# Five down products of block one in full float32, with their weights split a block later

## The chip, the core and the metric

The kernel runs on one core of a Trainium2 chip. The core has TensorE (PE, with its weight loads as PEld), VectorE (DVE), ScalarE (ACT), GpSimd (POOL) and SyncE (SP, whose queue issues most transfers). The metric is the device time of one execution in microseconds, and the median over several runs is compared.

## The reference

2048 tokens of 448 channels go through a conditioned state-space layer and a gated feed-forward layer, each with a residual:

```python
mod = (_silu(c) @ w_mod).reshape(c.shape[0], 6, 1, -1)
sa, ca, ga, sb, cb, gb = (mod[:, 0], mod[:, 1], mod[:, 2], mod[:, 3], mod[:, 4], mod[:, 5])
h = _layernorm(x, axis=-1) * (1 + ca) + sa
x = x + ga * _A_ref(h, ...)          # long convolution over the tokens, as a state-space kernel
h = _layernorm(x, axis=-1) * (1 + cb) + sb
x = x + gb * _B_ref(h, B_w_gate, B_w_up, B_w_down)
...
def _B_ref(x, w_gate, w_up, w_down):  # 448 -> 1792 -> 448
    g = _silu(x @ w_gate)
    u = x @ w_up
    return (g * u) @ w_down
```

Nearly all arithmetic is in `_B_ref`.

## The kernel before

**Products in parts.** The matmuls take operands in a reduced float32 format (F32R, "fp32r" in the profile). To keep float32 accuracy, a value a is split into a high part (a cast by ACT) and a low part (a minus the high part, a subtraction on DVE), and a product is the sum of three matmuls: high by high, high by low, low by high.

**Blocks and pieces.** After a first stage of about 34 us, which computes the modulation and the first tiles of the state-space layer, the 16 tiles of 128 tokens are worked off in eight blocks of two tiles (`run_blocks`, `ffn`). A block runs over 14 pieces f of the 1792 hidden channels, 128 each. Piece f consists of
- the gate and up products (`gate_up`): 42 matmuls with 256 columns, 64 rows each; gate runs on the upper half of the array's rows and up on the lower half, in pairs. The weights of a piece stand as a tile `gu` with a high and a low half; the activations as `hhi` and `hlo`. In block one the order is high by high, high weights by low activations, and the low weights last;
- the gating: ACT's Silu writes `p`, DVE multiplies it by the up product (into the PSUM bank), ACT casts the result to `phi`, DVE subtracts for `plo`;
- the down product (`down`): six slots, three for each of the two tiles, of 64 rows by 448 columns on each half of the array. It is asked for one half in the following piece and the other half in the piece after that (`begin`, `half`, `rest`); `point(f)` puts both between the gate and up matmuls of piece f, before the last two of them (in pieces 1 to 12 of block one).

**Weights in block one.** Gate and up weights of piece j (448 KB) are loaded into one of three staging tiles `raw`, j modulo 3 (`load_w`). `split_w(j, 0)` is ACT's cast into the high half, issued in the gating of piece j-2; the low half follows by `split_w(j, 1)`, a subtraction on DVE at the end of piece j-2. For the pieces in `ADDED` (5, 7, 9, 11, 13) the low half is made another way, `split_w(j, 2)` in the gating of piece j-3: ACT writes the negated weights' copy, and then POOL issues a transfer that adds the staging tile to it and rounds on the way. Hence the low half costs DVE nothing there. Note that the high half must be cast as well:

```python
if fresh and f + 3 in ADDED:
    split_w(f + 3, 2)
if nw is not None:
    split_w(nw, 0)
```

with `nw` = f + 2 in block one, which `fresh` marks. Down weights (224 KB a piece) go through three tiles `rawd` into `wdh` (ACT's cast) and `wdl` (DVE's subtraction, in the gating of their own piece). All split weights stay in SBUF for blocks two to eight, which load no weights.

**Order around it.** Each engine works off its instructions in the order in which they are issued. `PLANS` sets, for each block, after which piece the steps of the next block's tiles are issued: letters are steps (a, b, r, h, v: the convolution's operands; c, p: POOL's skip product and skip addition, at L1005 and L1008; u, w, m, M: statistics of the second norm; X, Y: normalising; T: transposition and stores to DRAM; U: loads of the turned rows into staging tiles), and digits the tile in the block. A plus puts steps inside the gating. In block one tile 0's `c0` stands after piece 4, `c1` and `p0` after piece 5, `p1` after piece 7, T1 after piece 10 and U1 after piece 12. The turned rows become the next block's `hhi` and `hlo` (`split_turned`).

Of the kernel before, what the change touches and what calls it, by code (L numbers as in the profile page):

```python
# [18 lines left out]
L, D, N, F = 2048, 448, 256, 1792  # L19
# [4 lines left out]
NF = F // 128  # L24
# [3 lines left out]
NS = 3  # L28
# [3 lines left out]

ADDED = (5, 7, 9, 11, 13)
PLANS = (
    """pre: s0 ; mid: t0 R0 f s1 ; a0 +g G ; b0 t1 ; r0 h0 R1 ; v0 a1 ; A0 b1 c0 ; B0 c1 e0 p0 ; r1 h1 v1 u0 w0 +E0 M0 ; X0 Y0 p1 ; A1 T0 ;
    B1 E1 m1 ; +M1 X1 Y1 T1 ; +U0 ; U1 e1 L0 ; L1""",
# [17 lines left out]
def f32(ap):  # L56
    return ap.bitcast(F32)
# [3 lines left out]
def tile_kernel(ctx, tc, x, a_re, a_im, b_re, b_im, c_re, c_im, log_dt,  # L61
                wd, wgate_up, states, groups, vecs, dft, idft, out):
    nc = tc.nc
    sy, ve, sc, po, pe = nc.sync, nc.vector, nc.scalar, nc.gpsimd, nc.tensor
# [50 lines left out]
    def split_d(j, part=None):  # L115
        hi, lo = wp[j]
        if not part:
            sc.copy(hi, wdn[j])
        if part != 0:
            ve.tensor_tensor(lo, wdn[j], f32(hi), op=OP.subtract)  # L120

    def split_w(j, part):
        w = raw[j]
# [13 lines left out]
    end = slice(96, 128)  # L137
# [62 lines left out]
    n1, n2 = Norm("a"), Norm("b")  # L200
# [60 lines left out]
    wp0 = ctx.enter_context(tc.tile_pool(name="wp0", bufs=1))  # L261
# [38 lines left out]
    with tc.tile_pool(name="pre", bufs=1) as pre:  # L300
# [4 lines left out]
        for kind, q in ((n[0], n[1:]) for n in ORDER.split()):  # L305
            if kind == "s":
                S[q] = pre.tile([128, NS_], F32, name="s" + q)
                sy.dma_start(S[q], states["abcdef".index(q)])
            elif kind == "m":
                g, b = int(q[0]), (slice(0, 2 * D), slice(2 * D, NM))[int(q[1])]  # L310
                if g not in wms:
                    wms[g] = pre.tile([128, NM], F32, name=f"wm{g}")
                sy.dma_start(wms[g][:, b], groups[g][:, b])
            else:
                {"x": load_x, "w": lambda j: load_w(wp0, j), "d": lambda j: load_d(wp0, j)}[kind](int(q))
        ar, ai, br, bi, cr, ci = (S[q] for q in "abcdef")


# [44 lines left out]
        t1, t2, t3, t4 = (pre.tile([128, NS_], F32, name=q) for q in ("t1", "t2", "t3", "t4"))  # L363
# [117 lines left out]
        def flag_of():  # L481
# [4 lines left out]
        k0, k1 = CV[:, 0:D], DN[2][:, 0:D]  # L486
# [45 lines left out]
            "d00": do(split_d, 0, 0),  # L532
# [212 lines left out]

    def run_blocks(pools, stages, first=None):
        work, hid = pools.work, pools.hid
        rest, ahead, leaving, gate_ready = [], [], [], []

        def both(top, low):  # L750

# [8 lines left out]
        def ffn(b, ts, fresh, last, todo):  # L760
            n, sums = 256, SUMS[b % 2]
            pp = {}
# [9 lines left out]
                return ps, [[(t[:, 0:n], *o) for t in ps] for o in ops]  # L772

            def gating(f, ps, nw):
                p = hid.tile([128, 256], F32, name="p") if fresh else p_of[f % 2]
                hi = hid.tile([128, 256], F32R, name="phi")
                lo = hid.tile([128, 256], F32R, name="plo")
                for g, a in todo.get(-2, []) if f == 0 else []:
                    g(*a)
                gate_ready[:] = [sc.activation(p, ps[0][:, 0:n], AF.Silu).ins.name]  # L780
# [17 lines left out]
                ve.tensor_tensor(lo, ps[1][:, 0:n], f32(hi), op=OP.subtract)  # L798
# [4 lines left out]
                if fresh:  # L803
                    sc.copy(wp[f + 1][0], wdn[f + 1])

            def down(f, q, z):

                hi, lo = pp[f]
                wh, wl = wp[f]
                u, v = ((hi, wh), (hi, wl), (lo, wh))[z]  # L810
                return sums[q][:, 0:D], u[:, cols(q)], v

            def begin(f):

                def half(c, fresh_, end):
                    return [[(*down(f, q, z), fresh_ and z == 0, end and z == 2) for z in range(3)] for q in (c, 1 - c)]

                rest.append((half(1 - f % 2, False, f == (NF - 3 if last else NF - 1)), [leave] if f == NF - 1 else None))
                return half(f % 2, f == 0, False)
# [92 lines left out]
                    pools.load(f + 2 + NS, f + NS)  # L912
            ahead[:] = [begin]

        for j in range(NP0, NP0 + NS - 1):
            pools.load(j)
        if first is not None:
# [18 lines left out]
        def steps(b, nx):  # L936
# [9 lines left out]
                  "o": lambda q: n1.stat(later[q], later), "O": lambda: n1.root(later), "G": gate_row, "g": gate_0, "f": first_rows,  # L946
# [203 lines left out]
```

## Time and profile before

| | us |
|---|---|
| median of 3 runs | 471.24 (471.05 to 471.61) |
| profiled execution, its own time | 471.01 |
| its span, first to last instruction | 469.0 |
| block one, first matmul to block two's first | 33.99 to 97.89 |
| PE busy over the span | 450.2 |
| DVE, ACT, POOL busy | 293.2, 163.6, 105.8 |
| mean granted clock of TensorE | 0.991 |

Busy time is what the instructions of an engine covered; matmuls overlap, so a busy PE is not necessarily at its peak. In rows of the timeline the first number is the start, the second the length, both in us; in square brackets stand the idle time of the engine just before and the engine that ended it. "x2" means that two neighbouring instructions are one row.

### The profile page before, as it was taken

The numbers are of one execution on the slowest core, as the hardware profiler recorded it, in microseconds if no ns is written. First come the engines' busy times: TensorE is split into PE (matmuls) and PEld (weight loads), VectorE is DVE, ScalarE is ACT, GpSimd is POOL, SyncE is SP. The second block draws the span as 40 slices with busy tenths as digits, with TensorE's granted clock in tenths as the row PEclk, the third lists the DMA queues.
The fourth block names the chain that finished last, engine by engine and source line by source line (L and its number), as shares of the span: only waits on it lengthen the run. The fifth ranks groups of instructions, "written<-read, shape, count | busy, mean of one in ns | idle before, by whom it ended". The sixth has DMA issues, their size and how long they took to land.

```text
span 469.0 us, 14543 instructions
## 1 busy us (share of the span) xinstructions
PE 450.2 (96%) x6355; PEld 430.5 (92%) x6355; DVE 293.2 (63%) x600; ACT 163.6 (35%) x395; POOL 105.8 (23%) x132
## 2 busy tenths in 40 slices
PE   6889979889999999999999999999999999999995
PEld 4548978889999999999999999999999999999995
DVE  4889878567664756656755657566755666443324
ACT  5876656442223322232223222232223222222211
POOL 1232423103600242022501142032401152000000
PEclk9999989899999999999999999999999999999999
DMA  8963857732022010302021011202021101202001
GB/s 305 407 231 100 246 160 193 197 77 79 3 61 60 22 61 21 101 1 81 2 74 48 28 55 40 82 3 81 2 81 41 41 4 47 74 3 77 9 1 45
DMA packets 19769, 38.01 MB, mean 81 GB/s; under 512 B 3313, under 2 KB 13169, under 8 KB 19697
## 3 DMA queue, kind: packets, MB, share of 16 engines
q1 hardware_dynamic: 18336, 34.53, 22.9%
q0 software_dynamic: 720, 2.29, 2.9%
q8 instruction: 51, 0.84, 0.7%
q10 hardware_dynamic: 640, 0.18, 0.2%
q14 instruction: 22, 0.17, 0.1%
HBM read 27.76 MB, written 6.88 MB: 74 GB/s over the span
## 4 chain that ended last, share of the span: by engine, by line
PE 81%; DVE 6%; DMA 4%; ACT 3%; issue 3%; POOL 1%; SPq 1%; DVEq 0%; POOLq 0%; ACTq 0%
PE bank L757 50%; PE dn L757 28%; DMA raw<-in_B_w_gate_up_dram 2%; DVE gu L127 1%; DMA raw<-xd 1%; DMA vec<-in_c_log_dt_dram 1%; DVE bank L792 1%; PE dn L489 1%; SPq L252 1%; ACT gu L125 1%; ACT gu L129 1%; DVE sta L161 0%; PE dn L856 0%; PE dn L389 0%; POOL rsa L190 0%
## 5 line engine op out<-in xcount | busy, mean ns | idle before, releaser
L757 PE MATMUL bank<-hhi,gu 64*128 64x256 f32 x3136 | 230.6, 276 | 7.4 <-DVE gu L127 3.7
L757 PEld LDWEIGHTS bank<-hhi,gu 64*128 64x128 f32 x3136 | 210.6, 185 | 9.7 <-DVE gu L127 4.3
L757 PE MATMUL bank<-hlo,gu 64*128 64x256 f32 x1568 | 137.3, 276 | 0.0
L757 PEld LDWEIGHTS bank<-hlo,gu 64*128 64x128 f32 x1568 | 123.0, 186 | 0.3
L780 ACT ACTIVATE raw<-bank 128x256 f32<-128x256 f32 x98 | 37.7, 385 | 190.1 <-PE bank L757 190.1
L792 DVE TENSOR_TENSOR bank<-raw,bank 128x256 f32<-128x256 f32 x91 | 38.9, 427 | 99.9 <-ACT raw L780 99.9
L757 PE MATMUL dn<-wdh,phi 64*128 64x448 f32 x440 | 93.1, 365 | 0.2 <-ACT p L780 0.2
L757 PE MATMUL dn<-wdh,plo 64*128 64x448 f32 x440 | 92.8, 363 | 0.0
L757 PE MATMUL dn<-wdl,phi 64*128 64x448 f32 x440 | 92.6, 362 | 0.0
L798 DVE TENSOR_TENSOR plo<-bank,phi 128x256 fp32r<-128x256 f32 x104 | 44.0, 423 | 29.5 <-ACT phi L797 29.5
L797 ACT CAST phi<-bank 128x256 fp32r<-128x256 f32 x104 | 38.8, 373 | 66.1 <-DVE bank L792 66.1
L757 PEld LDWEIGHTS dn<-wdh,plo 64*128 64x128 f32 x440 | 53.7, 186 | 2.4 <-DVE plo L798 1.4
L757 PEld LDWEIGHTS dn<-wdh,phi 64*128 64x128 f32 x440 | 53.5, 186 | 2.4 <-ACT phi L797 0.7
L757 PEld LDWEIGHTS dn<-wdl,phi 64*128 64x128 f32 x440 | 53.7, 186 | 0.4
L983 POOL TENSOR_TENSOR m<-m,gm 128x448 f32<-128x448 f32 x12 | 13.9, 1156 | 78.2 <-issue 44.2
L190 POOL TENSOR_SCALAR rsa<-mva 128x2 f32<-128x2 f32 (+1 forms) x10 | 6.1, 609 | 89.9 <-DVE mva L162 89.2
L190 POOL TENSOR_SCALAR rsb<-mvb 128x1 f32<-128x1 f32 x16 | 3.5, 219 | 75.4 <-DVE mvb L162 74.8
L259 DVE TENSOR_TENSOR hlo<-raw,hhi 128x512 fp32r<-128x512 f32 (+1 forms) x28 | 16.3, 622 | 2.3 <-ACT hhi L258 1.4
L1005 POOL TENSOR_TENSOR m<-m,gd 128x448 f32<-128x448 f32 x14 | 16.5, 1204 | 0.0
L127 DVE TENSOR_TENSOR gu<-raw,gu 128x896 fp32r<-128x896 f32 x9 | 13.4, 1489 | 3.0 <-ACT gu L125 3.0
L258 ACT CAST hhi<-raw 128x512 fp32r<-128x512 f32 (+1 forms) x28 | 14.6, 565 | 1.5 <-DMA raw<-xd 1.5
L216 DVE SCALAR_TENSOR_TENSOR m<-m,rsb,sb 128x448 f32<-128x448 f32 x14 | 13.8, 983 | 0.8
(214 smaller groups left out, 446.2 us busy)
## 6 DMA issues: line engine op xcount, KB each, us to landing
raw<-in_B_w_gate_up_dram SPq DMA_DIRECT2D x14, 448.0 KB, 3.6
raw<-xd SPq DMA_DIRECT2D x28, 224.0 KB, 3.6
rawd<-in_B_w_down_dram SPq DMA_DIRECT2D x16, 224.0 KB, 3.9
xd<-m SPq DMA_DIRECT2D x56, 56.0 KB, 1.7
x<-in_A_u_dram SPq DMA_DIRECT2D x12, 224.0 KB, 2.7
out_dram<-x SPq DMA_DIRECT2D x11, 224.0 KB, 2.0
wm<-in_w_mod_groups_dram SPq DMA_DIRECT2D x5, 448.0 KB, 8.2
gu<-raw POOLq DMA_DIRECT2D x5, 448.0 KB, 5.8
```

Source lines behind the costliest of these rows:

```text
L127: ve.tensor_tensor(wgu[j][:, 1], w, f32(wgu[j][:, 0]), op=OP.subtract)
L190: po.tensor_scalar(rs[:, 0:n], self.mv[:, 0:n, 1], EPS, None, op0=OP.add)
L216: ve.scalar_tensor_tensor(to, to, rs, sb, op0=OP.mult, op1=OP.add)
L258: sc.copy(hi, src)
L259: ve.tensor_tensor(lo, src, f32(hi), op=OP.subtract)
L757: done.append(pe.matmul(o, w[e], r[e], start=start, stop=stop).ins)
L780: gate_ready[:] = [sc.activation(p, ps[0][:, 0:n], AF.Silu).ins.name]
L792: ve.tensor_tensor(ps[1][:, 0:n], p, ps[1][:, 0:n], op=OP.mult)
L797: sc.copy(hi, ps[1][:, 0:n])
L798: ve.tensor_tensor(lo, ps[1][:, 0:n], f32(hi), op=OP.subtract)
L983: en.tensor_tensor(v, h, g, op=OP.mult)
L1005: po.tensor_tensor(h, h, gd, op=OP.mult)
```

## The change

Pieces 4, 6, 8, 10 and 12 (`WHOLE`) are computed in block one without splitting their down operands. DVE writes their gated product back into `p`, in float32, and the down product is one float32 matmul for each tile and array half, with the weights as they were loaded. Their weights have a tile of their own each, so that they stay until block two. There the new step `W` (`split_whole`) splits them, ACT's cast and DVE's subtraction, after pieces 2, 3, 5, 7 and 9, before the first use in pieces 5, 7, 9, 11 and 13. `ADDED` is empty: the low halves of pieces 5, 7, 9, 11 and 13 are made by DVE like the others, at the end of piece j-2. `p` of block one stands in one tile of its own with two places. The other staging tiles of down weights are counted over the nine remaining pieces.

```diff
-ADDED = (5, 7, 9, 11, 13)
+ADDED = ()
+WHOLE = (4, 6, 8, 10, 12)
...
-    """d0 R0 a0 b0 d1 R1 ; +l0 r0 h0 k0 ; +l1 v0 k1 ; A0 a1 b1 c0 ; B0 p0 e0 E0 c1 ; r1 h1 m0 M0 p1 ; +v1 X0 Y0 L0 L1 ; A1 T0 U0 ; B1 E1 m1 M1 ; +X1 Y1 T1 U1 ; e1 ; ; o0 ; o1 O""",
+    """d0 R0 a0 b0 d1 R1 ; +l0 r0 h0 k0 ; +l1 v0 k1 W4 ; W6 A0 a1 b1 c0 ; B0 p0 e0 E0 c1 ; W8 r1 h1 m0 M0 p1 ; +v1 X0 Y0 L0 L1 ; W10 A1 T0 U0 ; B1 E1 m1 M1 ; W12 +X1 Y1 T1 U1 ; e1 ; ; o0 ; o1 O""",
...
     def load_d(pool, j):
-        wdn[j] = stage_d[j % NS]
-        wp[j] = [pool.tile([128, D], F32R, name=f"wd{q}{j}") for q in "hl"]
+        if j in WHOLE:
+            wp[j] = [pool.tile([128, D], F32R, name=f"wdh{j}")]
+            wdn[j] = pool.tile([128, D], F32, name=f"wd{j}", tag="whole", bufs=len(WHOLE))
+        else:
+            wp[j] = [pool.tile([128, D], F32R, name=f"wd{q}{j}") for q in "hl"]
+            wdn[j] = stage_d[[k for k in range(NF) if k not in WHOLE].index(j) % NS]
...
+    def split_whole(pool, j):
+        a = dict(tag="spare") if j == WHOLE[0] else dict(tag="whole", bufs=len(WHOLE))
+        wp[j].append(pool.tile([128, D], F32R, name=f"wdl{j}", **a))
+        split_d(j)
...
-                p = hid.tile([128, 256], F32, name="p") if fresh else p_of[f % 2]
+                whole = fresh and f in WHOLE
+                if fresh and f == 0:
+                    first_p.append(pools.w.tile([128, 2, 256], F32, name="p", tag="spare"))
+                p = first_p[0][:, f % 2] if fresh else p_of[f % 2]
...
-                ve.tensor_tensor(ps[1][:, 0:n], p, ps[1][:, 0:n], op=OP.mult)
-                if fresh:
+                ve.tensor_tensor(p if whole else ps[1][:, 0:n], p, ps[1][:, 0:n], op=OP.mult)
+                if fresh and not whole:
                     split_d(f, 1)
...
-                sc.copy(hi, ps[1][:, 0:n])
-                ve.tensor_tensor(lo, ps[1][:, 0:n], f32(hi), op=OP.subtract)
+                if whole:
+                    pp[f] = p,
+                else:
+                    sc.copy(hi, ps[1][:, 0:n])
+                    ve.tensor_tensor(lo, ps[1][:, 0:n], f32(hi), op=OP.subtract)
...
-                if fresh:
+                if fresh and f + 1 not in WHOLE:
                     sc.copy(wp[f + 1][0], wdn[f + 1])
...
-                hi, lo = pp[f]
-                wh, wl = wp[f]
-                u, v = ((hi, wh), (hi, wl), (lo, wh))[z]
+                hi, lo = pp[f][0], pp[f][-1]
+                wh, wl = wp[f][0], wp[f][-1]
+                u, v = ((hi, wh), (hi, wl), (lo, wh))[z] if len(pp[f]) > 1 else (hi, wdn[f])
```

In the new order line numbers are 9 to 19 higher. First, DVE in block one from the end of piece 3 to piece 5 (`gu_609` before and `gu_608` after are piece 6's weights; `gu_539` piece 5's; L983 or L1002 is step b1, L798 or L813 a hidden value's low part). Before:

```order
L207 SCALAR_TENSOR_TENSOR m_77<-m_77,rsa,sa 128x448
L792 TENSOR_TENSOR bank<-p,bank 128x256
L120 TENSOR_TENSOR wdl_612<-rawd_80,wdh_611 128x448
L798 TENSOR_TENSOR plo<-bank,phi 128x256
L983 TENSOR_TENSOR m_77<-m_77,gm_88 128x448
L983 TENSOR_TENSOR v_844<-m_77,g_87 128x448
L127 TENSOR_TENSOR gu_609<-raw,gu_609 128x896
L792 TENSOR_TENSOR bank<-p,bank 128x256
```

And with the change:

```order
L216 SCALAR_TENSOR_TENSOR m_77<-m_77,rsa,sa 128x448
L136 TENSOR_TENSOR gu_539<-raw,gu_539 128x896
L804 TENSOR_TENSOR p<-p,bank 128x256
L1002 TENSOR_TENSOR m_77<-m_77,gm_88 128x448
L1002 TENSOR_TENSOR v_833<-m_77,g_87 128x448
L136 TENSOR_TENSOR gu_608<-raw,gu_608 128x896
L804 TENSOR_TENSOR bank<-p,bank 128x256
```

Piece 5's subtraction is new ahead of piece 4's gated product; piece 4's two splits are gone between that product and step b1.

Second, ACT in block one from the gating of piece 10 to that of piece 11 (`gu_1180` before and `gu_1139` after are piece 13's weights, `gu_1095` and `gu_1064` piece 12's). Before:

```order
L780 ACTIVATE p<-bank 128x256
L797 CAST phi<-bank 128x256
L129 ACTIVATE gu_1180<-raw 128x896
L125 CAST gu_1095<-raw 128x896
L804 CAST wdh_1182<-rawd_81 128x448
L780 ACTIVATE p<-bank 128x256
L797 CAST phi<-bank 128x256
L125 CAST gu_1180<-raw 128x896
```

And with the change:

```order
L792 ACTIVATE p<-bank 128x256
L134 CAST gu_1064<-raw 128x896
L819 CAST wdh_1141<-rawd_80 128x448
L792 ACTIVATE p<-bank 128x256
L812 CAST phi<-bank 128x256
L134 CAST gu_1139<-raw 128x896
```

The negation of piece 13's weights no longer stands ahead of piece 12's cast, and piece 10, being whole, has no cast of its hidden values.

Third, PE in block one at the point of piece 6: the second half of piece 4's down product and the first half of piece 5's. Before:

```order
L757 MATMUL dn_68<-wdh_611,phi 128x448 x2
L757 MATMUL dn_68<-wdl_612,phi 128x448 x2
L757 MATMUL dn_68<-wdh_611,plo 128x448 x2
L757 MATMUL dn_68<-wdh_692,phi 128x448 x2
L757 MATMUL dn_68<-wdl_693,phi 128x448 x2
L757 MATMUL dn_68<-wdh_692,plo 128x448 x2
```

And with the change:

```order
L766 MATMUL dn_68<-wd_611,p 128x448 x2
L766 MATMUL dn_68<-wdh_688,phi 128x448 x2
L766 MATMUL dn_68<-wdl_689,phi 128x448 x2
L766 MATMUL dn_68<-wdh_688,plo 128x448 x2
```

Three pairs of piece 4 have become one pair in float32.

More of the change, by code (lines that the diff above doesn't have):

```diff
@@ L31 @@
 MB = 3
-ADDED = (5, 7, 9, 11, 13)
+ADDED = ()
+WHOLE = (4, 6, 8, 10, 12)
 PLANS = (
-    """pre: s0 ; mid: t0 R0 f s1 ; a0 +g G ; b0 t1 ; r0 h0 R1 ; v0 a1 ; A0 b1 c0 ; B0 c1 e0 p0 ; r1 h1 v1 u0 w0 +E0 M0 ; X0 Y0 p1 ; A1 T0 ;
-    B1 E1 m1 ; +M1 X1 Y1 T1 ; +U0 ; U1 e1 L0 ; L1""",
[1 row of a table removed]
[2 rows of a table added]
     """a0 b0 ; +l0 k0 r0 h0 ; +l1 k1 v0 ; A0 a1 b1 c0 ; B0 p0 e0 E0 c1 ; r1 h1 m0 M0 p1 ; +v1 X0 Y0 L0 L1 ; A1 T0 U0 ; B1 E1 m1 M1 ; +X1 Y1 T1 U1 ; e1 ; o0 ; o1 O ;""",
@@ L314, in tile_kernel @@
             else:
-                {"x": load_x, "w": lambda j: load_w(wp0, j), "d": lambda j: load_d(wp0, j)}[kind](int(q))
+                {"x": load_x, "w": lambda j: load_w(wp0, j), "d": lambda j: j in WHOLE or load_d(wp0, j)}[kind](int(q))
         ar, ai, br, bi, cr, ci = (S[q] for q in "abcdef")
@@ L531, in tile_kernel @@
             "w0": do(split_w, 0, 0), "w01": do(split_w, 0, 1), "w1": do(split_w, 1, 0), "w11": do(split_w, 1, 1),
-            "d00": do(split_d, 0, 0),
+            "d00": lambda: 0 in WHOLE or split_d(0, 0),
             "rv": lambda: fits.append(nc.values_load(flag[0:1, 0:1], min_val=0, max_val=1)),
@@ L747, in run_blocks @@
         work, hid = pools.work, pools.hid
-        rest, ahead, leaving, gate_ready = [], [], [], []
+        rest, ahead, leaving, gate_ready, first_p = [], [], [], [], []
         def both(top, low):
@@ L791, in gating @@
                     return
-                ve.tensor_tensor(ps[1][:, 0:n], p, ps[1][:, 0:n], op=OP.mult)
-                if fresh:
+                ve.tensor_tensor(p if whole else ps[1][:, 0:n], p, ps[1][:, 0:n], op=OP.mult)
+                if fresh and not whole:
                     split_d(f, 1)
@@ L815, in half @@
                 def half(c, fresh_, end):
-                    return [[(*down(f, q, z), fresh_ and z == 0, end and z == 2) for z in range(3)] for q in (c, 1 - c)]
+                    n = 1 if len(pp[f]) < 2 else 3
+                    return [[(*down(f, q, z), fresh_ and z == 0, end and z == n - 1) for z in range(n)] for q in (c, 1 - c)]
                 rest.append((half(1 - f % 2, False, f == (NF - 3 if last else NF - 1)), [leave] if f == NF - 1 else None))
@@ L913, in ffn @@
             ahead[:] = [begin]
+        for j in (0, 1, 2):
+            if j in WHOLE:
+                load_d(pools.w, j)
         for j in range(NP0, NP0 + NS - 1):
@@ L945, in steps @@
                   "T": lambda q: turn(nx[q], q), "U": turned_back, "L": lambda q: load_x(later[q]), "l": lambda q: leaving[0](q, 0), "k": lambda q: leaving[0](q, 1),
-                  "o": lambda q: n1.stat(later[q], later), "O": lambda: n1.root(later), "G": gate_row, "g": gate_0, "f": first_rows,
+                  "o": lambda q: n1.stat(later[q], later), "O": lambda: n1.root(later), "G": gate_row, "W": lambda *j: split_whole(pools.w, int("".join(map(str, j)))), "g": gate_0, "f": first_rows,
                   **{k: each(g) for k, g in st.items()}}
```

1 line of the change is left out of this document (removed), and 1 row of the table PLANS.

## The prediction

> **What bounds the kernel now.** I read the busy tenths first (40 slices of the span), then busy time by stage (columns: length, then busy time and instructions of PE, weight load, DVE, ACT, POOL, then granted clock, DMA share, GB/s).
>
> ```profile
> PE   6889979889999999999999999999999999999995
> 34.00:102.00 68.00, 60.84 (x822) 56.92 (x824) 52.65 (x91) 40.74 (x83) 16.03 (x23) 0.95 0.63 170
> 102.00:154.00 52.00, 51.88 (x773) 50.44 (x771) 33.72 (x71) 14.62 (x37) 13.93 (x16) 1.00 0.16 46
> ```
>
> From the tenth slice on, TensorE has no slice below nine tenths but the last: it is the bound there. Block two fills its 52 us but for 0.12; block one takes 68 us, with 7 us of PE idle and a lower clock. So block one can give time back, and nothing else can. What a piece costs undisturbed is seen in the chain of waits of block two (12 down matmuls, then 42 gate and up matmuls); the PE timeline gives block one's waits, and the stages around the two longest give the clock (in those rows the clock stands third from the end).
>
> ```profile
> 142.58 1.20 PE dn L757 x12
> 143.78 2.39 PE bank L757 x42
> 33.99 1.87 PE L757 MATMUL bank<-hhi,gu 64*128 64x256 f32 x28 [0.39 <-issue]
> 42.78 0.97 PE L757 MATMUL bank<-hhi,gu 64*128 64x256 f32 x12 [0.64 <-DVE gu L127]
> 60.86 1.62 PE L757 MATMUL bank<-hhi,gu 64*128 64x256 f32 x12 [2.49 <-DVE gu L127]
> 69.20 0.96 PE L757 MATMUL bank<-hlo,gu 64*128 64x256 f32 x14
> 74.79 0.95 PE L757 MATMUL bank<-hlo,gu 64*128 64x256 f32 x14
> 87.28 1.10 PE L757 MATMUL bank<-hhi,gu 64*128 64x256 f32 x14 [1.81 <-ACT gu L125]
> 97.89 1.21 PE L757 MATMUL bank<-hhi,gu 64*128 64x256 f32 x16 [1.45 <-ACT hhi L258]
> 60.86:64.44 3.58, 3.58 (x25) 0.52 0.63 191
> 88.20:91.70 3.50, 3.50 (x36) 0.51 1.04 185
> 96.40:102.00 5.60, 4.15 (x57) 1.00 0.32 85
> ```
>
> Fourteen pieces of 2.39 + 1.20 are 50.3 us; less 1.8 for the down products that pieces 0 and 1 lack, plus 0.33 for each of four convolution groups and 0.75 for the gate row, block one would need 50.6. It runs from 33.99 to 97.89, 63.9 us: 13.3 are lost. Piece 2 loses 0.64; piece 6 2.49, and 1.7 more because the clock is half for 3.4 us right after; piece 8 1.7 (its lo products and the next piece's start 5.59 apart, 3.93 would be even pace); piece 12 1.81 and again 1.7 of half clock; the first matmul of block two 1.45. That is 11.5. The other 1.8 are crumbs, of which I lay 0.3 to each half-clock stretch. The wait of 1.45 is followed by full clock.
>
> Next, what was late at each place.
>
> ```profile
> 55.03 0.62 DVE L983 TENSOR_TENSOR v<-m,g 128x448 fp32r<-128x448 f32 x1
> 56.10 4.71 DVE L127 TENSOR_TENSOR gu<-raw,gu 128x896 fp32r<-128x896 f32 x1 [0.45 <-ACT gu L125]
> 69.60 1.08 DVE L127 TENSOR_TENSOR gu<-raw,gu 128x896 fp32r<-128x896 f32 x1
> 55.55 0.93 POOL L130 DMA_DIRECT2D gu<-raw  x1 [5.26 <-ACT gu L129]
> 56.19 2.58 POOL L1005 TENSOR_TENSOR m<-m,gd 128x448 f32<-128x448 f32 x2
> 58.40 1.44 POOL L1008 TENSOR_TENSOR x<-m,x 128x448 f32<-128x448 f32 x1
> 85.45 0.95 ACT L129 ACTIVATE gu<-raw 128x896 fp32r<-128x896 f32 x1 [2.34 <-DMA raw<-in_B_w_gate_up_dram]
> 86.31 0.92 ACT L125 CAST gu<-raw 128x896 fp32r<-128x896 f32 x1
> 85.66 1.74 SPq L248 DMA_DIRECT2D xd<-m  x4
> raw<-xd SPq DMA_DIRECT2D x4, 224.0 KB, 6.3
> raw<-xd SPq DMA_DIRECT2D x28, 224.0 KB, 3.6
> ```
>
> At piece 6 the low half of the weights is one DVE subtraction, which takes 4.71 us instead of 1.08: three POOL operations run beside it, and it ends 0.97 after the last of them (59.84). All its operands are in SBUF. At piece 12, ACT has piece 13's negation ahead of piece 12's cast in its queue, and that waits for piece 13's weights. At the end the turned rows of block one take 6.3 us to land, against 3.6 as the median of the whole run, while the DMA engines are full (share 1.04 above).
>
> **The change, part by part.** *Transfers and negations.* Five ACT negations (0.95 each), five POOL issues (0.93) and five adding transfers of 448 KB go; five DVE subtractions of 1.08 come, for pieces 5, 7, 9, 11 and 13. No load is added, and SP's queue holds the same issues in the same order. In ACT's order, piece 12's cast no longer stands behind anything of piece 13. The wait of 1.81 goes, with it the half clock and 0.3 of crumbs: 3.8 saved.
>
> *What the whole pieces drop.* Each drops one DVE subtraction of weights, one of hidden values, and an ACT cast of each.
>
> ```profile
> 61.06 0.61 DVE L120 TENSOR_TENSOR wdl<-rawd,wdh 128x448 fp32r<-128x448 f32 x1
> 67.49 0.41 DVE L798 TENSOR_TENSOR plo<-bank,phi 128x256 fp32r<-128x256 f32 x1
> 62.29 0.57 ACT L804 CAST wdh<-rawd 128x448 fp32r<-128x448 f32 x1
> 64.82 0.39 ACT L780 ACTIVATE p<-bank 128x256 f32<-128x256 f32 x1 [1.41 <-PE bank L757]
> 71.48 0.36 ACT L780 ACTIVATE p<-bank 128x256 f32<-128x256 f32 x1
> 69.69 1.08 POOL L182 TENSOR_SCALAR cs<-mvb 128x1 f32<-128x1 f32 x1 [1.59 <-ACT m L181]
> 72.51 1.34 POOL L1008 TENSOR_TENSOR x<-m,x 128x448 f32<-128x448 f32 x1
> 73.08 1.25 DVE L214 SCALAR_TENSOR_TENSOR m<-x,mvb,cbw 128x448 f32<-128x448 f32 x1
> ```
>
> With 0.08 off each for the overlap of neighbours, DVE loses 5 x (0.54 + 0.34) = 4.4 and gains 5 x 1.0 = 5.0. It is busy 52.65 of 68, so the sum fits, but its order matters.
>
> Piece 6: without the issues on its queue, POOL does tile 0's skip product as soon as tile 1's norm is done, some 9 us earlier, beside the DVE list of piece 2. It can hold up piece 4's subtraction by its own 1.29 at most, where PE showed no wait; I take nothing. Piece 6's subtraction no longer waits for ACT: it follows at once on the product that ends at 55.65, while POOL's next operation waits for that product's semaphore, so DVE is first and ends near 56.7. PE asked at 60.86 - 2.49 = 58.37. The 2.49, the 1.7 and 0.3 of crumbs go: 4.5 saved. POOL's two operations then hold the next SBUF subtraction, piece 5's down weights, to about 59.7, when PE needs it near 60.
>
> Piece 8: piece 7's Silu comes 6.66 us after piece 6's, behind tile 0's statistics (POOL's 1.08 is in that chain). Two DVE operations (0.54 + 0.34) leave the chain, but piece 6's product now waits about 0.7 for piece 7's new subtraction. Bounds are all 1.7 and 0.8; I keep 1.2, so 0.5 saved.
>
> Piece 9: its subtraction is new on DVE, behind piece 7's product (0.34) and two splits (0.54, 0.34) and two normalising steps of some 0.7, the first of which POOL's addition holds up by 0.7 (the 1.25 row, ending 0.48 after POOL's). With its own 1.0 that is 4.3 from the end of piece 7's Silu. PE, held by the same Silu, needs it after 0.75 + 0.60 + 0.33 + 0.11 + 1.6 = 3.4. Lost 0.8; between 0 and 1.4.
>
> *Full float32 products.* The trace has two calls of this shape, 64 rows by 448 columns in float32, at the gate row; the reduced ones of piece 3 stand below them.
>
> ```profile
> 36.48 0.56 PE L738 MATMUL dn<-gb,pick 64*128 64x448 f32 x2
> 36.85 0.56 PE L738 MATMUL dn<-gb,pick 64*128 64x448 f32 x2
> 37.23 0.33 PEld L757 LDWEIGHTS bank<-hhi,gu 64*128 64x128 f32 x4 [0.17 <-issue]
> 47.18 0.37 PE L757 MATMUL dn<-wdh,phi 64*128 64x448 f32 x2
> 47.38 0.37 PE L757 MATMUL dn<-wdl,phi 64*128 64x448 f32 x2
> 47.58 0.37 PE L757 MATMUL dn<-wdh,plo 64*128 64x448 f32 x2
> ```
>
> Two calls become four instructions, two by two, and PE goes on after 37.23 - 36.48 = 0.75. Three reduced pairs take 0.20 each, 0.60. A whole piece has two such slots: 10 x 0.15 = 1.5 us lost, all on PE's path. [...]
>
> *The end of block one.* The stores of tile 1's turned rows began at 85.66, and block two 12.23 later. They move forward by 4.2 (pieces 6, 8 and 9), back by 1.05 (seven slots before them), forward by 0.88 (what piece 10 drops): 81.6. From there 1.74 for the stores, five more issues of 0.44, 3.6 to land, 0.7 for the cast, 8.3, and 0.3 in hand: 90.2. Piece 13 ended at 97.89 - 1.45 = 96.44 and moves by 8.0 forward and 1.5 back, to 89.9. A wait of 0.3 where 1.45 was: 1.15 saved. At worst all 12.23 stay.
>
> *Block two* gets five ACT casts (0.57) and five DVE subtractions (0.61). Both engines have room there (14.62 and 33.72 of 52), and each split is asked for pieces later. Bounds 0 and 1.0; I take 0.3.
>
> **Sum.** Saved 4.5 + 3.8 + 0.5 + 1.15 = 9.95; lost 1.5 + 0.8 + 0.3 = 2.6; net 7.35. The profiled execution took 471.01 (span 469.0), 0.23 below the median of 471.24; from the median it is 463.9.
>
> **Rivals.** *A, the return path.* The last chain keeps its 12.23: block two starts at 93.8, 3.6 later than forecast, and a wait of nearly 4 us brings a half clock, 1.7: 469.2. For it: that chain is transfers, and SP's queue is unchanged. Against: the adding transfer that ran beside it is gone.
>
> *B, the lock.* POOL's two remaining operations (1.29 and 1.44) get ahead of piece 6's subtraction, as they did before: it ends at 59.4 and PE waits 1.0: 464.9.
>
> *C, DVE becomes the bound.* The other four new subtractions are each exposed like piece 9's, 0.9 apiece: 467.5. For it: 52.65 of busy time in a block that shrinks to 56. Against: in pieces 5, 11 and 13 little else stands in its list.
>
> *D, slower.* The four instructions of a slot do not overlap at all; each lasts about 0.53, so 2.14 a slot. Ten slots cost 13.9 more, of which 2.3 fill the waits left at pieces 8, 9 and the end: 475.5. It decides from 1.71 a slot. Against it stand the starts at 36.48, 36.85 and 37.23.
>
> *E, the clock.* The half clock does not come from the waits, and both stretches stay: 463.9 + 3.4 = 467.3. Both stretches begin right behind the two longest waits, which speaks against it. [...]
>
> **Chances.** Forecast 0.60 (own range 462 to 466), A 0.10, B 0.12, C 0.08, E 0.03, D 0.05, no effect at all 0.02. Below, if the waits at 8, 9 and the end vanish and block two costs nothing: 463.9 - 2.6 = 461.3. Above, 468.5 takes in B, C and E and leaves out A's worst. A measurement of this kernel tells 0.2% from no change: faster 0.92, within 0.03, slower 0.05.
>
> **What would show it.** Right: no matmul of pieces 6 and 12 with a wait over 1 us, clock 1.00 through block one, subtractions of gate and up weights at 1.1 us each, float32 slots of 0.75, block two beginning near 90. Wrong: such a subtraction at 2 us or more beside POOL, PE waiting on DVE at pieces 5, 7, 11 or 13, turned rows landing in over 5 us, float32 slots over 1 us, or gaps in block two.

## The result and the profile after

| | before | after |
|---|---|---|
| median, four runs each, us | 471.43 (471.05 to 471.61) | 466.02 (464.95 to 466.29) |
| profiled execution, own time | 471.01 | 466.29 |
| its span | 469.0 | 464.5 |
| block one, first matmul to block two's first | 63.90 | 57.53 |

The ratio is 0.9882, 95% interval 0.9865 to 0.9899: 5.4 us faster, where 7.35 were forecast. In a second group of runs on one chip it was 465.63 against 470.18, 0.9897 (0.9868 to 0.9927), so 4.6 to 5.4 us. The 466.02 lies inside the stated range (461.3 to 468.5) and at the upper edge of the forecast's own (462 to 466).

The busy tenths and the stages of the changed kernel, in the columns used before:

```profile
PE   7789999899999999999999999999999999999995
34.00:100.00 66.00, 62.07 (x855) 55.37 (x855) 53.86 (x93) 34.27 (x72) 13.43 (x19) 1.00 0.46 145
100.00:152.00 52.00, 51.42 (x770) 49.69 (x768) 36.08 (x76) 16.94 (x42) 14.35 (x18) 1.00 0.17 46
```

One slice of block one is still below nine tenths, the eighth, and the clock stands at 1.00 through both rows. DVE is busier in block one's row than before (53.86 of a shorter stretch), and block two has 0.58 us of PE idle where it had 0.12.

TensorE's timeline: its start in block one, and the longest waits from there on:

```profile
35.08 1.87 PE L766 MATMUL bank<-hhi,gu 64*128 64x256 f32 x28 [0.40 <-issue]
43.99 0.97 PE L766 MATMUL bank<-hhi,gu 64*128 64x256 f32 x12 [0.68 <-DVE gu L136]
72.55 0.97 PE L766 MATMUL bank<-hhi,gu 64*128 64x256 f32 x12 [0.42 <-DVE gu L136]
92.61 1.18 PE L766 MATMUL bank<-hhi,gu 64*128 64x256 f32 x16 [2.26 <-ACT hhi L267]
119.40 0.47 PE L766 MATMUL dn<-wdh,phi 64*128 64x448 f32 x2 [0.44 <-ACT phi L812]
```

The waits of pieces 6 and 12 are gone; piece 2's 0.68 was 0.64 before. What is left is one large wait, and it stands at the start of block two, where I forecast 0.3. Block one also starts 1.09 later than in the profile of before (33.99). The start differs between executions: in the six further profiles with float32 pieces it lay between 33.55 and 35.02, in the six further ones without between 33.72 and 34.72.

VectorE and GpSimd around piece 6, where the subtraction had taken 4.71 us:

```profile
56.56 1.09 DVE L136 TENSOR_TENSOR gu<-raw,gu 128x896 fp32r<-128x896 f32 x1
56.73 1.93 POOL L1024 TENSOR_TENSOR m<-m,gd 128x448 f32<-128x448 f32 x1 [7.62 <-DVE v L1002]
58.62 1.15 POOL L1027 TENSOR_TENSOR x<-m,x 128x448 f32<-128x448 f32 x1
58.92 1.33 DVE L124 TENSOR_TENSOR wdl<-rawd,wdh 128x448 fp32r<-128x448 f32 x1
```

The subtraction comes first and takes 1.09, and GpSimd's product beside it takes 1.93, where the other tile's took 1.20 (47.90). Then GpSimd's sum comes first, takes 1.15, and VectorE's split of 0.61 takes 1.33. In these two pairs the one that starts first goes at its own speed and the other is held. In the profile before, the subtraction's record (56.10) also begins 0.09 ahead of GpSimd's product (56.19), but GpSimd's issue of the adding transfer was running then (55.55, 0.93 long), and the subtraction was held through all three (4.71).

A float32 slot (first row) with a reduced pair behind it, and the start of the pair after that:

```profile
84.96 0.91 PE L766 MATMUL dn<-wd,p 64*128 64x448 f32 x4
85.36 0.72 PE L766 MATMUL dn<-wdh,phi 64*128 64x448 f32 x2
85.92 0.36 PE L766 MATMUL dn<-wdl,phi 64*128 64x448 f32 x2
```

From 84.96 to 85.92 are 0.96 us; less 0.20 for the reduced pair, a slot is 0.76, as forecast from the gate row.

The end of block one: the transposition before (first row), then with the change transposition, stores and loads of the turned rows, conversions.

```profile
84.99 0.65 DVE L246 STREAM_TRANSPOSE m<-m 128x448 f32<-128x448 f32 x1
82.02 0.65 DVE L255 STREAM_TRANSPOSE m<-m 128x448 f32<-128x448 f32 x1
82.69 1.74 SPq L257 DMA_DIRECT2D xd<-m  x4
85.00 2.46 SPq L261 DMA_DIRECT2D raw<-xd  x4
89.43 0.62 ACT L267 CAST hhi<-raw 128x512 fp32r<-128x512 f32 x1 [1.19 <-DMA raw<-xd]
91.94 0.62 ACT L267 CAST hhi<-raw 128x512 fp32r<-128x512 f32 x1 [1.89 <-DMA raw<-xd]
```

From the end of the transposition, 82.67, to block two's first matmul are 9.94 us. It was 12.25 before (85.64 to 97.89) and 8.6 in the forecast. Both tiles' conversions wait for a load.

### The profile page after: what moved, and what is told of

Read it like the earlier page. It is cut to its first block, busy times and chain, and to the rows that moved or that the text cites. A ratio compares the mean times of both kernels' runs of the same rounds, so it can differ in the third digit from the quotient of the medians.

```text
span 464.5 us, 14489 instructions
## 1 busy us (share of the span) xinstructions
PE 447.6 (96%) x6335; PEld 425.9 (92%) x6335; DVE 294.2 (63%) x600; ACT 157.5 (34%) x385; POOL 102.7 (22%) x127
## 4 chain that ended last, share of the span: by engine, by line
PE 81%; issue 5%; DVE 5%; ACT 3%; POOL 3%; DMA 2%; SPq 0%; POOLq 0%; DVEq 0%; ACTq 0%
PE bank L766 50%; PE dn L766 27%; DMA x<-in_A_u_dram 1%; DMA raw<-xd 1%; DVE gu L136 1%; ACT gu L134 1%; PE dn L498 1%; DVE bank L804 1%; POOL m L1002 0%; POOL rsa L200 0%; POOL v L1002 0%; PE dn L872 0%; PE dn L398 0%; DVE m L223 0%; ACT phi L812 0%
## 5 line engine op out<-in xcount | busy, mean ns | idle before, releaser
L766 PE MATMUL bank<-hhi,gu 64*128 64x256 f32 x3136 | 227.4, 275 | 3.8 <-ACT hhi L267 2.3
L766 PEld LDWEIGHTS bank<-hhi,gu 64*128 64x128 f32 x3136 | 206.9, 184 | 6.8 <-ACT hhi L267 2.8
L766 PE MATMUL bank<-hlo,gu 64*128 64x256 f32 x1568 | 134.0, 275 | 0.0
L766 PEld LDWEIGHTS bank<-hlo,gu 64*128 64x128 f32 x1568 | 119.8, 184 | 0.2
L766 PE MATMUL dn<-wdh,phi 64*128 64x448 f32 x420 | 87.2, 366 | 0.4 <-ACT phi L812 0.4
L766 PE MATMUL dn<-wdh,plo 64*128 64x448 f32 x420 | 86.2, 362 | 0.0
L766 PE MATMUL dn<-wdl,phi 64*128 64x448 f32 x420 | 85.8, 359 | 0.0
L813 DVE TENSOR_TENSOR plo<-bank,phi 128x256 fp32r<-128x256 f32 x99 | 41.9, 423 | 29.5 <-ACT phi L812 29.5
L766 PEld LDWEIGHTS dn<-wdh,phi 64*128 64x128 f32 x420 | 48.5, 184 | 3.3 <-ACT phi L812 1.5
L766 PEld LDWEIGHTS dn<-wdh,plo 64*128 64x128 f32 x420 | 48.6, 184 | 1.8 <-DVE plo L813 0.8
L766 PEld LDWEIGHTS dn<-wdl,phi 64*128 64x128 f32 x420 | 48.9, 184 | 0.9 <-issue 0.6
L1002 POOL TENSOR_TENSOR m<-m,gm 128x448 f32<-128x448 f32 x12 | 13.9, 1155 | 78.9 <-issue 43.8
```

Of the source, the lines that this page charges most:

```text
L766: done.append(pe.matmul(o, w[e], r[e], start=start, stop=stop).ins)
L1002: en.tensor_tensor(v, h, g, op=OP.mult)
```

## The experiments

Theory 1 at the start: the gain comes from removing the adding transfers and negations, which made two waits; float32 products cost TensorE a little and make room on VectorE. Theory 2: the float32 pieces carry the gain. All times below are medians. The kernel before, on the same chip and beside the group, was at 470.43, 470.18 and 470.40 in the three groups.

The mean granted clock of an execution tells how many stretches of half clock it had, since one takes 0.0036 off (half of 3.41 us in about 468) and the fall of the clock at the very end up to 0.0025 (0.0020 in the profile before, from 467.11 on). The profiles without a stretch have 0.998 to 1.000, those with one 0.994 to 0.996, the one with two 0.991. I count 0.990 to 0.993 as two.

### No adding transfers, no float32 pieces

```diff
-ADDED = (5, 7, 9, 11, 13)
+ADDED = ()
```

made in the kernel before.

> The kernel before, with no adding transfers: the low halves of pieces 5, 7, 9, 11 and 13 are made by DVE, nothing else is changed. Theory 1 (the gain comes from removing the adding transfers and the negations that stand in ACT's queue; the float32 pieces only make room on DVE and cost 1.5 us of PE): most of the gain is there already, the waits of 2.49 and 1.81 and both half-clock stretches are gone, and DVE, with 5 x 1.0 us more and nothing dropped, gives back 1 to 3 us at pieces 8, 9 and the end of block one: about 467.5 (466.5 to 469). Theory 2 (the float32 pieces carry the gain, because DVE could not take the five subtractions without them): no gain, 470.5 or more.

Measured 468.14 (466.52 to 470.27), ratio 0.9954 (0.9932 to 0.9976): 2.3 us faster. TensorE's wait at block two, with the stage behind it (the clock stands third from the end):

```profile
93.13 1.89 PE L757 MATMUL bank<-hhi,gu 64*128 64x256 f32 x16 [2.67 <-ACT hhi L258]
82.63 0.65 DVE L246 STREAM_TRANSPOSE m<-m 128x448 f32<-128x448 f32 x1
93.37:96.79 3.42, 3.42 (x31) 3.30 (x30) 2.97 (x8) 1.44 (x5) 0.00 (x0) 0.50 0.28 79
```

The two waits are gone here too. The transposition ends at 83.28, 49.36 after block one's start at 33.92; with float32 pieces it is 47.59. This execution also paid half clock at the start of block two.

### Float32 pieces, with the adding transfers kept

```diff
-ADDED = ()
+ADDED = (5, 7, 9, 11, 13)
```

made in the changed kernel.

> The changed kernel, with the adding transfers kept for pieces 5, 7, 9, 11 and 13: the float32 pieces alone. Theory 1: the waits of PE at pieces 6 and 12 stay, each over 1.5 us and followed by half clock, the ten float32 slots cost 1.5 us, the dropped splits give back 0.5 to 1: about 471.5 (470 to 473), as the kernel before. Theory 2: about 467, most of the gain.

Measured 470.24 (468.95 to 470.46), ratio 0.9991 (0.9979 to 1.0004): no gain.

```profile
55.66 4.70 DVE L136 TENSOR_TENSOR gu<-raw,gu 128x896 fp32r<-128x896 f32 x1 [1.31 <-ACT gu L134]
60.42 0.96 PE L766 MATMUL bank<-hhi,gu 64*128 64x256 f32 x12 [2.29 <-DVE gu L136]
56.43:59.85 3.42, 1.70 (x30) 1.50 (x27) 3.42 (x1) 0.38 (x1) 2.97 (x3) 1.00 0.72 139
59.85:63.26 3.41, 2.84 (x34) 2.42 (x36) 2.34 (x5) 2.10 (x4) 0.00 (x0) 1.00 0.52 143
90.57:93.98 3.41, 1.02 (x20) 0.83 (x16) 1.15 (x3) 1.33 (x3) 0.00 (x0) 1.00 0.61 170
93.98:97.39 3.41, 3.41 (x28) 3.00 (x30) 3.10 (x8) 1.62 (x5) 0.00 (x0) 0.50 0.11 43
```

The held subtraction and its wait are back, at 4.70 and 2.29. That settles the first theory against the second: float32 pieces alone, with the transfers kept, bring nothing that can be measured. Two things were not foreseen. The wait at piece 12 did not come back, although piece 13's negation stands ahead of piece 12's cast again: piece 13's weights landed earlier here, so that the negation began 47.95 after block one's start (81.50 less 33.55), against 51.46 before (85.45 less 33.99), and the cast behind it was done in time. So the order in ACT's queue makes a wait only when that load lands late. And the wait of 2.29 has no half clock behind it, while the 2.38 at block two has; the last section takes that up.

### One adding transfer less: piece 7, or piece 13

```diff
-ADDED = (5, 7, 9, 11, 13)
+ADDED = (5, 9, 11, 13)
```

> The kernel before, with piece 7 alone taken out of the adding transfers. Theory 1 (at piece 6 it is the order: ACT's negation of piece 7 holds the cast of piece 6, and the transfer's issue holds POOL, so that POOL's three operations get ahead of DVE's subtraction): piece 6's subtraction takes 1.1 us, the wait of 2.49 and the half clock behind it are gone, piece 12's stay: about 467.3 (466.5 to 469). Rival (the clock does not follow from the wait): only 2.5 less, 469. Rival (POOL and DVE meet at the next place instead): 470.5 or more, with another subtraction of over 2 us.

Measured 468.27 (467.07 to 469.98), ratio 0.9949 (0.9927 to 0.9970): 2.2 us less, nearer to the first rival's 2.5 than to the first theory's drop of about 4. By the granted clock, 7 of these 10 executions still had half clock somewhere (0.993 to 0.996). Piece 6's wait is gone, piece 12's is there:

```profile
83.72 1.07 PE L757 MATMUL bank<-hhi,gu 64*128 64x256 f32 x14 [2.21 <-ACT gu L125]
79.92:83.34 3.42, 1.59 (x20) 1.24 (x16) 1.72 (x3) 1.45 (x2) 0.14 (x1) 1.00 0.31 101
83.34:86.75 3.41, 3.03 (x48) 2.99 (x50) 2.29 (x4) 2.66 (x6) 0.81 (x1) 1.00 0.69 149
```

```diff
-ADDED = (5, 7, 9, 11, 13)
+ADDED = (5, 7, 9, 11)
```

> The kernel before, with piece 13 alone taken out of the adding transfers. Theory 1: ACT's negation no longer stands ahead of piece 12's cast, the wait of 1.81 and the half clock behind it are gone, 3.5 us. But tile 1's turned rows start no earlier (85.7 on the clock of the profile before), and take about 9.9 us as in the changed kernel: block two starts near 95.6 instead of 97.9, so only about 2.3 of the 3.5 reach the end: about 469 (468 to 470), with a wait of 2 to 4 us at block two's first matmul. Rival (that return path is not the limit): 467.8.

Measured 468.67 (468.09 to 469.23), ratio 0.9967 (0.9953 to 0.9981): 1.8 us less. Here it is the other way round:

```profile
60.79 0.98 PE L757 MATMUL bank<-hhi,gu 64*128 64x256 f32 x12 [2.50 <-DVE gu L127]
58.91:62.32 3.41, 1.53 (x20) 1.49 (x22) 3.03 (x4) 1.21 (x3) 0.87 (x1) 1.00 0.32 58
62.32:65.74 3.42, 3.42 (x32) 3.31 (x30) 2.18 (x4) 2.50 (x6) 0.00 (x0) 0.50 0.46 169
```

Each wait goes with the transfer that the prediction named for it, piece 7's for the first and piece 13's for the second. A removal takes away the negation, the issue on POOL and the transfer at once; which of the three makes the wait is read from their order in the traces, and no run separates them. Each is worth about 2 us, not the 4.5 and 3.8 of my sum.

### Both of these, and nothing else

```diff
-ADDED = (5, 7, 9, 11, 13)
+ADDED = (5, 9, 11)
```

> The kernel before with the adding transfers of pieces 7 and 13 alone taken out. Taken out one by one these gave 2.2 and 1.8 us. Theory 1 (the two waits are separate, each with its half clock): they add, 466.5 us (465.5 to 467.5). Theory 2 (VectorE, which makes the splits instead, and the return path take it back, as they seem to with all five out, 468.1 us): 467.6 to 468.7 us.

Measured 466.38 (465.65 to 466.59), ratio 0.9915 (0.9898 to 0.9931): 4.0 us, the sum of 2.2 and 1.8. This version of the kernel before, without a single float32 piece and with three adding transfers left, lies within 0.4 to 0.8 us of the changed kernel, and block one takes 57.53 in its profile, as long as in the changed kernel's.

```profile
82.10 0.65 DVE L246 STREAM_TRANSPOSE m<-m 128x448 f32<-128x448 f32 x1
92.25 1.18 PE L757 MATMUL bank<-hhi,gu 64*128 64x256 f32 x16 [1.66 <-ACT hhi L258]
```

Its transposition ends 48.03 after block one's start at 34.72, against 47.59. Taking the other three transfers away as well gives VectorE three more subtractions, and the time was 468.14, 1.8 more than this (in another group).

### The changed kernel again

> The changed kernel once more, as the yardstick of this group. Both theories: 466.0 us (465.0 to 466.6), 0.9 to 1.2% under the kernel before. They differ on the clock. Theory 1 (window): the clock is set in fixed windows of 3.41 us whose phase differs from one execution to the next, and a window in which TensorE stood for about 1.8 us or more is followed by one at half clock; the one wait of that size that is left, 2.26 us at the start of block two, falls far enough inside one window in some 6 of 10 executions, so the times of single executions lie up to 1.7 us apart. Theory 2 (each wait of 1.8 us or more is followed by half clock): the 2.26 us would have been followed by a stretch of 0.50, which the profile of it does not have.

Measured 465.63 (464.27 to 467.15), ratio 0.9897 (0.9868 to 0.9927).

```profile
92.46 1.19 PE L766 MATMUL bank<-hhi,gu 64*128 64x256 f32 x16 [3.15 <-ACT hhi L267]
87.23:90.64 3.41, 2.08 (x26) 1.52 (x22) 1.32 (x2) 0.75 (x2) 0.00 (x0) 1.00 0.73 179
90.64:94.05 3.41, 1.59 (x26) 1.59 (x28) 1.57 (x4) 1.03 (x3) 0.00 (x0) 1.00 0.34 96
94.05:97.46 3.41, 3.41 (x46) 2.65 (x44) 1.95 (x6) 1.69 (x5) 0.00 (x0) 1.00 0.00 0
```

The longest wait of all profiles from block one on has no half clock behind it: a border of the 3.41 us windows that the last section counts cuts it into 1.33 and 1.82. The return path took 10.85 here (81.61 to 92.46), 0.9 more than in the first profile, and the runs spread over 2.9 us, more than the 1.7 of one half-clock stretch that I had expected. So the return path varies too. Half clock was rarer than the expectation's 6 in 10: of the ten executions of the changed kernel, in both groups, 7 had none (0.998 to 1.000) and 3 had some (0.993 to 0.996).

### The first tile's rows loaded earlier

```diff
-... B1 E1 m1 ; +M1 X1 Y1 T1 ; +U0 ; U1 e1 L0 ; L1
+... B1 E1 m1 ; +M1 U0 X1 Y1 T1 ; ; U1 e1 L0 ; L1
```

U0 is the load of the first tile's turned rows, T1 the second tile's transposition and stores.

> The first tile's turned rows are loaded ahead of the second tile's stores at the end of block one. Theory 1 (the return path at the end of block one is what my forecast made 1.3 us too short, and it is long because both tiles' loads come back behind the second tile's stores): the wait ahead of block two's first matmul falls from 2.26 to about 1.0 us, and the time by 1.0 to 1.5 us, to 464.8 us (464.0 to 465.5); half clock there no longer, since 1.0 us cannot fill half of a window. Theory 2 (the path is the second tile's own chain, transposition, store, load, conversion, which the first tile's does not lengthen): no change, 466.0 us (465.5 to 466.5), the first tile's conversions earlier and the last one where it was.

Measured 463.42 (462.92 to 465.45), ratio 0.9864 (0.9835 to 0.9894): 2.2 us less than the changed kernel of the same group, more than expected.

```profile
79.02 1.14 SPq L261 DMA_DIRECT2D raw<-xd  x2
80.74 0.65 DVE L255 STREAM_TRANSPOSE m<-m 128x448 f32<-128x448 f32 x1
88.53 0.62 ACT L267 CAST hhi<-raw 128x512 fp32r<-128x512 f32 x1 [0.86 <-DMA raw<-xd]
89.20 1.21 PE L766 MATMUL bank<-hhi,gu 64*128 64x256 f32 x16
```

The second tile's own path shrinks from 9.94 to 7.81 (81.39 to 89.20), although it still holds the same steps: two loads instead of four go out behind the stores. TensorE no longer waits. The gain is about the size of the wait of 2.26.

The same move in the kernel before:

> The kernel before with the first tile's turned rows loaded ahead of the second tile's stores, the move that took 2.2 us from the changed kernel. Theory 1 (the return path is the bound at the end of block one in the changed kernel, where piece 13 ends earlier, and in the kernel before it is only just so): the 1.45 us wait there goes, 1.0 to 1.5 us less than the kernel before: 469.0 us (468.3 to 469.8). Theory 2 (in the kernel before the adding transfers hold the loads back, whatever their order): no change, 470.2 us (469.6 to 470.8).

Measured 468.92 (467.73 to 470.82), ratio 0.9970 (0.9953 to 0.9986): 1.5 us less, as the first theory had it. It does not become free of waits there, since piece 13's gate and up products now wait for an adding transfer:

```profile
92.80 0.73 PE L757 MATMUL bank<-hhi,gu 64*128 64x256 f32 x8 [1.12 <-DMA gu<-raw]
```

And with no adding transfers, without float32 pieces (the edit of the first experiment and this one):

> The kernel before with no adding transfers, all its pieces split on VectorE, and the first tile's turned rows loaded early; against the changed kernel with the same move, 463.4 us, it lacks only the float32 pieces. Without the move the two stood at 468.1 and 466.0 us. Theory 1 (float32 products bring their 2 us by making room on VectorE inside block one, whatever the return path does): 465.6 us (464.8 to 466.4). Theory 2 (they brought it at the end of block one alone, where the float32 kernel waited 2.3 us and this one 2.7 us with half clock behind it): 463.5 to 464.5 us.

Measured 465.54 (464.86 to 466.56), ratio 0.9897 (0.9876 to 0.9918), where the first theory expected 465.6.

```profile
82.40 0.65 DVE L246 STREAM_TRANSPOSE m<-m 128x448 f32<-128x448 f32 x1
91.86 0.85 PE L757 MATMUL bank<-hhi,gu 64*128 64x256 f32 x10 [1.63 <-ACT hhi L258]
```

So float32 pieces are worth some 2 us where all subtractions are VectorE's: 2.1 with the move (465.54 to 463.42), 2.1 to 2.5 without it (468.14 to 466.02 or 465.63). Each of these pairs is taken across two groups; by the ratios it would be 1.6 with the move and 2.7 to 3.4 without. In the profiles with the move, block one is 2.69 shorter with float32 pieces: 1.69 by the time of the transposition, 49.33 after block one's start here and 47.64 there (80.74 + 0.65 - 33.75), and 1.00 by the path behind it, 8.81 and 7.81.

### Later splits in block two

```diff
-... k1 W4 ; W6 A0 a1 b1 c0 ; B0 p0 e0 E0 c1 ; W8 r1 h1 m0 M0 p1 ; ... ; W10 A1 T0 U0 ; B1 E1 m1 M1 ; W12 +X1 ...
+... k1 ; A0 a1 b1 c0 W4 ; B0 p0 e0 E0 c1 W6 ; r1 h1 m0 M0 p1 W8 ; ... ; A1 T0 U0 W10 ; B1 E1 m1 M1 ; +X1 Y1 T1 U1 W12 ; ...
```

> Block two's splits of the weights of pieces 4 to 12 are issued behind the convolution's steps of their pieces, not ahead of them. Theory 1 (the splits ahead of the second convolution step put GpSimd's chain 0.7 us back, which gave the 0.44 us wait at piece 6 of block two): that wait goes, 0.4 to 0.6 us less, 465.5 us (464.9 to 466.2). Theory 2 (the split's late end then delays the down products that use it, or the wait comes from elsewhere): same or up to 1 us more.

Measured 466.04 (464.64 to 467.31), ratio 0.9909 (0.9880 to 0.9939): no change, and the wait at piece 6 of block two stayed.

```profile
117.29 0.62 DVE L124 TENSOR_TENSOR wdl<-wd,wdh 128x448 fp32r<-128x448 f32 x1
117.82 0.42 DVE L804 TENSOR_TENSOR bank<-raw,bank 128x256 f32<-128x256 f32 x1
118.70 0.47 PE L766 MATMUL dn<-wdh,phi 64*128 64x448 f32 x2 [0.62 <-ACT phi L812]
```

The chain through GpSimd did come 0.35 earlier (L1059 begins 24.96 after block two's start, against 25.31), but now a split itself stands right ahead of VectorE's gated product, on which the cast that TensorE waits for depends. Theory 2 had the time right; its mechanism was another, since it is not the down products using the split that wait.

### The moves together

The two moves above, and the first tile's two normalising steps of block one (X0 and Y0) a piece later; the expectation calls them skip steps, but `p1`, GpSimd's skip addition, stays where it was:

```diff
-... X0 Y0 p1 ; A1 T0 ; ...
+... p1 ; X0 Y0 A1 T0 ; ...
```

> The two moves above together, and the third one: the first tile's two skip steps of block one a piece later, so that GpSimd no longer holds VectorE's copy at piece 9 (0.42 us wait). Theory 1: the three add, 2.0 to 2.4 us less than the changed kernel, 463.8 us (463.0 to 464.6). Theory 2 (each one's gain is taken up by the next chain): 465.5 us or more.

Measured 462.90 (462.50 to 464.30), ratio 0.9848 (0.9821 to 0.9876), the fastest of all. It is 0.5 below the earlier load alone, whose interval it overlaps. The wait of 0.42 at piece 9 is gone and the transposition ends 46.91 after the start instead of 47.64, but then the return path is last again:

```profile
89.02 1.19 PE L766 MATMUL bank<-hhi,gu 64*128 64x256 f32 x16 [0.44 <-ACT hhi L267]
```

### Each float32 slot twice

```diff
-                    n = 1 if len(pp[f]) < 2 else 3
+                    n = 2 if len(pp[f]) < 2 else 3
```

> The changed kernel with each float32 down product of the five pieces issued twice, so that their sum comes out doubled: ten slots more of 0.75 us by the changed kernel's profile, 7.5 us of TensorE work. Theory 1 (a float32 slot is on TensorE's path for its whole length): 1.5 us of it, the last of the five pieces, fall into the 2.26 us wait ahead of block two and some 0.6 us into the small waits; the rest is seen, 5.4 us (4.5 to 7.5) on 465.8 us: 471.2 us (470.3 to 473.3). Theory 2 (block one is held by VectorE or the return path, and the slots run beside it): under 2 us, 466 to 468 us.

Measured 468.45 (468.00 to 468.89), ratio 0.9954 (0.9937 to 0.9970): 2.4 to 2.8 us slower than the changed kernel, below the first theory's range and above the second's. Both missed.

```profile
69.89 1.67 PE L766 MATMUL dn<-wd,p 64*128 64x448 f32 x8
70.00:90.00 20.00, 20.00 (x248) 16.57 (x244) 15.35 (x25) 7.59 (x14) 2.85 (x3) 1.00 0.51 159
95.33 1.08 PE L766 MATMUL bank<-hhi,gu 64*128 64x256 f32 x16
```

A slot grew from 0.91 to 1.67, and TensorE shows no wait from piece 2 to the end of block one. Nine of the ten slots lie ahead of block two's first matmul, 6.75 us, but block one grew by 2.78 only (35.02 to 95.33, against 57.53). Waits of 0.17, 0.42 and 2.26 took up 2.85. The other 1.1 I cannot assign to recorded waits. So TensorE's own work had 4 us of room in block one.

## Why the prediction was right in sign and short in size

Between the two profiles, the spans differ by 4.5, and by 5.6 without the later start. The forecast by the same steps was 7.4.

| step | forecast | measured |
|---|---|---|
| end of tile 1's transposition, from block one's start | -4.06 | -4.06 (51.65 to 47.59) |
| return path to block two's first matmul | -3.6 (to 8.6) | -2.3 (to 9.94) |
| block two to the end | +0.3 | +0.8 (371.1 to 371.9) |

- **Piece 6, piece 12, the lock.** Right in mechanism for this execution. The subtraction started first, its 4.71 became 1.09, both waits and the half clock went. Rival B did not occur; the later split was held, as the prediction said. The two single removals show which transfer each wait goes with. That the transposition moved by 4.06, as forecast to the hundredth, is luck: in two other profiles with the wait at piece 6, without piece 13's transfer and with the early load, it ended 50.59 and 51.37 after block one's start, not 51.65.
- **The size of these two.** Over many runs they are worth 2.2 and 1.8, added up 4.0, not 8.3. Both stretches of half clock, 3.4 us of the 8.3, were in the one execution that I had profiled. By the granted clock, all 50 executions of the kernel before in the three groups had at least one, but only 24 had two or more (0.989 to 0.993), and those took 0.7 us longer in the median than the other 26 (470.95 against 470.25), not 1.7. So 1.7 a stretch was too much: the time lost at half clock is in part made up at later waits, which I read from these medians and no run shows directly. Likewise a wait removed is partly given to the next one: without piece 7's transfer piece 12 waited 2.21 instead of 1.81, piece 13 a new 0.99 for an adding transfer, and block two 2.44 instead of 1.45.
- **The return path, the step that failed.** "From there 1.74 for the stores, five more issues of 0.44, 3.6 to land, 0.7 for the cast" was short in two terms. The last load issue ended 4.79 after the transposition, where 1.74 and 2.2 make 3.94: the four loads took 2.46 and gaps stood around the issue between. And from there to the last cast's start 4.48 passed, where I took the run's median landing of 3.6. In seven other profiles with this order of loads, in which TensorE waited for its end, the path was between 9.50 and 13.13. Rival A's mechanism was there to a third of its price: the path was 1.3 longer than forecast, not 3.6, with a wait of 2.26, not nearly 4.
- **Piece 13** ended at 90.35, 0.64 earlier than forecast once the later start is allowed for.
- **Float32 slots.** The length was right, 0.76. The 1.5 us that I laid on TensorE's path were too much, if the doubled slots are a measure: some 2.8 of their 6.75 us were seen. Rival D was far off. What float32 pieces bring, some 2 us over splitting on VectorE, I had spread over pieces 8, 9 and the end without naming it.
- **Pieces 8 and 9.** At piece 8 the two low products stand 4.96 apart (66.22 and 71.18), 0.9 over an even pace with one float32 slot (3.93 + 0.15 = 4.08), where I kept 1.2. Piece 9's wait came as said, 0.42 and not 0.8, behind the normalising step that GpSimd held up.
- **Block two** took 0.8 longer, within the bounds of 0 and 1.0 that I gave: the wait of 0.44 at its piece 6 and crumbs. But without float32 pieces it took 371.4 to 371.9 as well (with piece 7's or piece 13's transfer out), so only the wait is surely the change's. Moving the splits did not take it away.
- **Rival E**, half clock that stays, was refuted for this execution, and for 7 of 10 of the changed kernel. What I did not have is that a wait alone is not enough: it has to fall far enough inside one of the 3.41 us windows that the last section counts: the 2.49 before left 0.92 us of TensorE's work in one, the 2.26 here left 1.70 and 2.87 in two.

## What to carry to other kernels

Take apart a change that does two things before crediting either: here two of five transfers carried 4.0 of the 4.6 to 5.4 us, and float32 pieces repaid what taking the other three away cost VectorE. When the waits inside a block go, ask what comes back last at its end, and price each issue and landing of that path by its own stage, not by the median of the run. Do not price a half-clock stretch from one profile: it comes by chance (24 of 50 executions of the kernel before had a second one), and over these executions the second one cost 0.7 us, not 1.7.

## What the runs showed of the hardware

The half clock was a surprise. It came in stretches of 3.41 us. In the profile before, two of them begin 27.31 us apart (60.92 and 88.23), which is eight times 3.41, and the clock falls for the last time at 467.11, 378.88 after the second, which is 111 times 3.413 to within 0.05; so I count windows of that length back and forth from a stretch, or from the fall of the clock at the very end of an execution. Windows of the kernel before that hold its two waits, and those behind them (busy time of TensorE stands first behind the length):

```profile
57.51:60.92 3.41, 0.92 (x18) 0.72 (x14) 3.41 (x2) 0.00 (x0) 2.33 (x3) 1.00 0.55 103
60.92:64.34 3.42, 3.42 (x24) 3.22 (x26) 1.71 (x4) 2.21 (x4) 0.00 (x0) 0.50 0.66 197
84.82:88.23 3.41, 1.60 (x24) 1.30 (x22) 1.75 (x3) 2.52 (x4) 0.95 (x1) 1.00 0.31 86
88.23:91.64 3.41, 3.41 (x34) 3.37 (x32) 1.33 (x4) 1.68 (x3) 0.00 (x0) 0.50 1.05 186
```

Both waits lie within one window. Of 14 waits of 1.8 us or more from block one on in these profiles, 6 were followed by half clock, and in each of the 6 TensorE was busy for 0.73 to 1.60 of one window's 3.41 us. The other 8 were cut by a border or too short: their emptiest windows had 1.59 or more, such as the 1.70 and 2.84 of the 2.29 us wait above, the 1.59 and 3.03 of the 2.21, and the 2.08 and 1.59 of the 3.15. Between 1.59 and 1.60 both happened, so in these profiles the edge lies near there, at a little under half (0.47 of 3.41). By that, a wait of length w between 1.8 and 3.4 is followed by half clock in about (w - 0.2) / 3.4 of executions, an estimate from these windows: 0.67 for 2.49, 0.47 for 1.81. It is on the high side, giving 9 of these 14 waits, and 6 in 10 for the changed kernel, which had 3 in 10. And the two chances of the kernel before are not independent: were they, some 9 of its 50 executions should have had no half clock, and none was without. A reading that would fit, and that no run shows: the two waits begin 27.1 us apart (58.37 and 85.47), close to eight windows, with a half clock between them; where the first wait escapes, that delay is missing, so the second begins up to 1.7 earlier against its window and mostly falls inside it.

No run here moved the windows on purpose; the relation is read off from where they happened to fall.
